# Packed attention and a mixture of experts on one core: the first matrix in 256-column chunks, quarters in the first beat

## The chip, the core and the metric

The kernel runs on one core of a Trainium2 chip. TensorE (PE in the profile, its weight loads PEld) multiplies, VectorE (DVE), ScalarE (ACT) and GpSimd (POOL) do the elementwise work, and SyncE (SP) issues nearly all DMAs from one queue. The metric is device microseconds of one execution, and the median of several runs is given.

## The reference

Each head's 32 "packed" queries `p` attend to 576 keys and values; then the 576 rows of `q` attend to the 32 packed rows. The result `x` (4608 tokens of 512 numbers, 8 batches of 576) goes through a mixture of 8 experts, one expert for each token.

```python
p_packed = sm_attn(p, k, v)               # 8 batches x 8 heads, 32 x 64 out
x = sm_attn(q, p_packed, p_packed)        # 8 x 8 x 576 x 64, heads side by side: 4608 x 512
logits = x @ w_gate; e_idx = argmax(logits)
gate_w = softmax(logits)[e_idx]; eom = sigmoid(x @ w_output_gate)
for e in range(8):
    mask = e_idx == e
    h = maximum(x[mask] @ w1[e], 0)       # 512 -> 1024
    out[mask] = gate_w * eom[mask, e] * (h @ w2[e])   # 1024 -> 512
```

## The kernel before

**A beat is a batch.** Since each `x` row is a weighted mean of 32 packed rows for each head, `x @ w1[e]` is never made from `x`: `values_up` multiplies the packed rows by the first matrix of the batch's commonest expert (`ps_G`, in the document G), and `ffn` multiplies the attention weights by G. Every operand is split into a high and a low part (`Gh`, `Gl`, `ah`, `al`, `w2h`, `w2l`), and a product is three matmuls. Tokens of the batch that chose another expert are marked and done later, in `quarters` and `first_leftover` (the left-over pass), which stages its own weights.

**The parts of a beat.** `encode` (scores `ps_s`, the sum over values `ps_pp`, its division `rs` and `ppc` on DVE, its transposition `ps_ppT` by PE, the expert's choice), `route` (scores of `q`, exponentials, `a2T`, the split into `ah` and `al`, the gate's logits `ps_lg`), `weights` (DMAs of the first matrix, tile `w`, four of 512 KB; of the second, tile `wst`, four of 512 KB; then for each of these an ACT cast to `w2h` and a subtraction to `w2l` on POOL or DVE), `values_up`, `ffn`. `ffn` has two halves: 256 tokens, then 320. In each, eight blocks of the 1024 hidden columns take six matmuls each into `ps_h`; ACT (L615) and DVE (L618) make `hT` from it; then `ps_o` is the product with the second matrix (L656, L671).

**The order is written by hand.** `ffn` of one batch is the backbone; `START` and, for each beat, a string of `PLANS` say after which of its steps a piece of another batch's `encode` (y, x, Y), `route` (t, r), `weights` (W, w), `values_up` (G, g) or of the left-over pass (l) is issued. Every engine runs its instructions in the order in which they are written, and so does SP's queue of DMAs. Before the first beat PE is kept busy by products of a blank tile (`warm`, `CFG["warm"]`, digits in `START`).

**Where the bounds come from.** PSUM has 8 banks in rotation: a new tile waits until the tile eight allocations before it is read. `by_head` and `beside` (L104) issue matmuls for four 32-row strips side by side. In the first beat G of 512 columns (a half) is made, split by ACT (`Gh`, L88) and DVE (`Gl`, L89), and the other half follows after two blocks of `ps_h`.

Of the kernel before, what the change touches and what calls it, by code (L numbers as in the profile page):

```python
# [22 lines left out]
           pool=("w2.2", "w3.3", "w4.3", "w5.3", "w6.3", "w7.3", "w3.0", "w4.0", "w5.0", "w6.0", "w7.0", "w0.0",  # L23
# [11 lines left out]
PLANS = ["0:kq 1:t 2:GGW 3:W 5:ty 6:W 7:tW 9:WWW 10:yW 11:tt 12:t 13:y 14:ytyy 15:qt 16:tyyyt 18:y "  # L35
# [5 lines left out]
        + [STEADY] * 2 + [  # L41
         "1:y 3:y 8:rxyr 9:Wyrrrrr 10:tqt 12:r 13:r 14:rr 15:yl 16:rw 17:wkl 18:v 19:vx 25:xx 26:lxwx "
         "29:l 30:kxw 31:wqgxgrlw 34:rrgwxwxwll",
         "1:yl 3:y 8:rxylr 9:Wyrrrrr 10:tqt 12:r 13:rl 14:rr 15:y 16:rw 17:wk 18:v 19:vx 25:xx 26:xwx "
         "30:kxw 31:wqgxgrlw 34:rrgwxwxw",
         "1:l 3:t 6:W 7:t 34:l"]

# [2 lines left out]
def tile_packed_attn_then_moe(ctx, tc, first_in, qT, kp, k2, v, w1, w2, out):  # L50
# [343 lines left out]
    def route(b):  # L394
# [40 lines left out]
        for part in ([0, 1],) if b else ([0], [1]):  # L435
            ts = slice(part[0] * HS, (part[-1] + 1) * HS)
            n = (ts.stop - ts.start) // NP
            sf = [x[:, ts] for x in rows]
            sv = [x.rearrange("p (j n) -> p j n", n=NP) for x in sf]
            sms = []  # L440
            for g in range(NG):
                mx = sb.tile([P, S // NP, 1], F32, tag="mx", name="mx", bufs=2)[:, :n]
                nc.vector.tensor_reduce(mx, sv[g], axis=AX.X, op=ALU.max)
                eng("sub", b, part[0], g).tensor_tensor(sv[g], sv[g], mx.to_broadcast([P, n, NP]), ALU.subtract)  # L444
                yield
            for g in range(NG):
# [118 lines left out]
    def values_up(b):  # L565

        w1s = W[b][0]
        ppT = packed[b]
        G[b] = []

        def up(n):
            banks = [bank("ps_G") for _ in range(NG)]
            by_head(banks, ppT, w1s[n * NPAIR:(n + 1) * NPAIR])
            return banks

        def take_in(banks):
            made = [[sb.tile([P, BANK], F32R, tag=x, name=x, bufs=4, **WIDE) for x in ("Gh", "Gl")] for _ in banks]
            step = BANK // 2 if b == 0 else BANK
            for x in range(0, BANK, step):
                for ps, (gh, gl) in zip(banks, made):  # L580
                    split(gh[:, x:x + step], gl[:, x:x + step], ps[:, x:x + step])
            G[b].extend(map(tuple, made))
# [141 lines left out]
    def leftover():  # L724
# [56 lines left out]
    def quarters(nb, m):  # L781
# [37 lines left out]
        vals = st([4], "l_valq")  # L819
        nc.vector.tensor_copy(vals, ps)  # L820
        ridi = row_ids(st, decf, vals, m)
        yield
        ps = bank("ps_l")[:, :NPAIR * m]
# [96 lines left out]
def _layout(q, k, v, p, moe_w_gate, moe_w_output_gate, moe_w1, moe_w2):  # L920
# [26 lines left out]
    def parts(x):  # L947
# [33 lines left out]
```

## Time and profile before

| | |
|---|---|
| median of 3 runs | 391.12 us (390.99 to 392.66) |
| the profiled execution, its own time | 389.64 us |
| span of its trace | 388.0 us |
| PE busy | 379.3 us, 98% of the span |
| DVE, ACT, POOL busy | 248.4, 186.2, 106.5 us |
| TensorE's granted clock | full in all 40 slices of the span |

The profiled execution is 1.6 us longer than its span and 1.5 us below the median. Busy times overlap and don't add up; PE's 98% says that its instructions follow one another nearly throughout. "Idle before" is time an engine stood still ahead of an instruction, with what released it; "issue" means that nothing that the profile shows was waited for. A wait of an engine other than PE costs only what it passes on.

### The profile page before, as it was taken

Reading aid. Unit: us, or ns where it says so; the run is one execution under the profiler, and the core shown is the slowest. Engines: PE = TensorE matmul, PEld = TensorE weight load, DVE = VectorE, ACT = ScalarE, POOL = GpSimd, SP = SyncE. Lnnn points to the kernel's source line nnn. Section 1 sums busy time; section 2 is a strip of 40 time slices with the busy share of each in tenths; the row PEclk is TensorE's granted clock in tenths of the full one; section 3 lists DMA queues with packets and bytes.
Section 4 is the critical chain, followed back from the end, with each engine's and each line's share of the span. In section 5 each row is a group of like instructions: output and inputs, shape, how many; then the busy total and the mean of one; then the engine's idle time right before and its main releaser. Section 6 shows DMA issues by size and latency. Waiting matters only on the chain.

```text
span 388.0 us, 9841 instructions
## 1 busy us (share of the span) xinstructions
PE 379.3 (98%) x3880; PEld 310.7 (80%) x3880; DVE 248.4 (64%) x703; ACT 186.2 (48%) x421; POOL 106.5 (27%) x92
## 2 busy tenths in 40 slices
PE   8799999999999999999999999999999999999996
PEld 3468886879769897798869898698968789788986
DVE  5778688775867973678646875559846594153250
ACT  2267444744395255734566346552476334552321
POOL 4534013232146021431044021340735101442000
PEclk9999999999999999999999999999999999999999
DMA  7899189909983499522894259712863948600101
GB/s 288 332 387 421 64 244 387 379 20 328 387 272 95 164 295 414 190 98 95 334 355 175 64 170 407 280 51 91 277 263 111 359 160 287 236 30 0 56 14 57
DMA packets 35535, 83.79 MB, mean 216 GB/s; under 512 B 3486, under 2 KB 15136, under 8 KB 35488
## 3 DMA queue, kind: packets, MB, share of 16 engines
q1 hardware_dynamic: 35024, 81.89, 57.9%
q10 hardware_dynamic: 432, 1.26, 0.8%
q8 instruction: 31, 0.51, 0.5%
q14 instruction: 16, 0.13, 0.1%
q0 software_dynamic: 32, 0.00, 0.0%
HBM read 67.93 MB, written 15.27 MB: 214 GB/s over the span
## 4 chain that ended last, share of the span: by engine, by line
PE 94%; DMA 3%; DVE 2%; issue 1%; ACT 0%; SPq 0%
PE ps_o L656 46%; PE ps_h L97 25%; PE ps_o L671 8%; PE ps_G L104 4%; PE ps_pp L104 3%; PE ps_s2T L104 2%; PE ps_s L104 2%; DMA w<-in_w_dram 2%; PE ps_lg L104 1%; PE warm L128 1%; DMA k<-in_first_dram 1%; PE ps_lo L853 0%; DVE a1T L333 0%; PE ps_ppT L352 0%; DVE nm L307 0%
## 5 line engine op out<-in xcount | busy, mean ns | idle before, releaser
L656 PE MATMUL ps_o<-w2h,hT 128*128 128x512 f32 (+1 forms) x528 | 165.7, 387 | 0.0
L656 PEld LDWEIGHTS ps_o<-w2h,hT 128*128 128x128 f32 x528 | 98.2, 188 | 22.8 <-issue 3.0
L656 PE MATMUL ps_o<-w2l,hT 128*128 128x512 f32 (+1 forms) x264 | 101.2, 383 | 0.0
L618 DVE SCALAR_TENSOR_TENSOR hT<-ps_h,hT 128x256 fp32r<-128x256 f32 x192 | 61.1, 352 | 53.9 <-ACT hT L615 53.2
L559 POOL TENSOR_TENSOR w2l<-wst,w2h 128x1024 fp32r<-128x1024 f32 x27 | 66.6, 2476 | 100.8 <-ACT w2h L557 97.5
L97 PE MATMUL ps_h<-ah,Gh 128*128 128x256 f32 (+1 forms) x256 | 77.1, 301 | 1.3 <-DVE hT L618 0.8
L97 PE MATMUL ps_h<-al,Gh 128*128 128x256 f32 (+1 forms) x256 | 75.7, 296 | 0.0
L97 PE MATMUL ps_h<-ah,Gl 128*128 128x256 f32 (+1 forms) x256 | 75.7, 296 | 0.0
L615 ACT ACTIVATE hT<-ps_h 128x320 fp32r<-128x320 f32 (+1 forms) x128 | 52.0, 414 | 39.4 <-PE ps_h L97 38.7
L656 PEld LDWEIGHTS ps_o<-w2l,hT 128*128 128x128 f32 x264 | 49.7, 188 | 9.0
L97 PEld LDWEIGHTS ps_h<-ah,Gh 128*128 128x128 f32 x256 | 48.5, 190 | 3.2 <-DVE hT L618 1.0
L97 PEld LDWEIGHTS ps_h<-al,Gh 128*128 128x128 f32 x256 | 48.5, 190 | 1.2 <-issue 0.7
L97 PEld LDWEIGHTS ps_h<-ah,Gl 128*128 128x128 f32 x256 | 48.5, 189 | 0.0
L557 ACT CAST w2h<-wst 128x1024 fp32r<-128x1024 f32 x32 | 33.3, 1063 | 7.0 <-DMA wst<-in_w_dram 7.0
L471 POOL TENSOR_TENSOR al<-a2T,ah 128x576 fp32r<-128x576 f32 (+1 forms) x10 | 14.2, 1423 | 81.0 <-ACT ah L468 80.9
L639 ACT ACTIVATE ob<-ps_o,scm_all 128x512 f32<-128x512 f32 (+1 forms) x28 | 19.1, 682 | 33.7 <-PE ps_o L656 33.2
L89 DVE TENSOR_TENSOR Gl<-ps_G,Gh 128x512 fp32r<-128x512 f32 (+1 forms) x36 | 20.9, 623 | 16.2 <-ACT Gh L88 15.9
L671 PE MATMUL ps_o<-w2h,hT 128*128 128x512 f32 x64 | 25.2, 393 | 0.0
L671 PE MATMUL ps_o<-w2l,hT 128*64 128x512 f32 x64 | 23.7, 391 | 0.0
L468 ACT CAST ah<-a2T 128x576 fp32r<-128x576 f32 (+1 forms) x18 | 11.1, 621 | 18.3 <-DVE a2T L462 18.3
L447 ACT ACTIVATE s<-s 128x576 f32<-128x576 f32 (+1 forms) x18 | 11.1, 629 | 16.6 <-DVE s L444 14.1
L88 ACT CAST Gh<-ps_G 128x512 fp32r<-128x512 f32 (+1 forms) x36 | 17.6, 542 | 2.2 <-PE ps_G L104 1.7
(175 smaller groups left out, 407.2 us busy)
## 6 DMA issues: line engine op xcount, KB each, us to landing
w<-in_w_dram SPq DMA_DIRECT2D x36, 512.0 KB, 5.8
wst<-in_w_dram SPq DMA_DIRECT2D x32, 512.0 KB, 9.1
vt<-in_v_dram SPq DMA_DIRECT2D x14, 650.0 KB, 11.5
q<-in_qT_dram SPq DMA_DIRECT2D x14, 576.0 KB, 4.6
out_dram<-ob SPq DMA_DIRECT2D x31, 256.0 KB, 2.3
a_d<-a2T SPq DMA_DIRECT2D x16, 320.0 KB, 3.1
k<-in_kp_dram SPq DMA_DIRECT2D x7, 640.0 KB, 6.8
k<-in_k_dram SPq DMA_DIRECT2D x7, 576.0 KB, 9.1
```

The costliest lines, as they stand in the source:

```text
L88: (hi_eng or nc.scalar.copy)(hi, src)
L89: (lo_eng or nc.vector).tensor_tensor(lo, src, f(hi), ALU.subtract)
L97: res = nc.tensor.matmul(dst, a, m, start=j == 0, stop=j == len(seq) - 1)
L104: res = nc.tensor.matmul(dst, a, m, start=j == 0, stop=j == len(seqs[0]) - 1)
L471: eng("al", b, part[0], g).tensor_tensor(al[:, g, ts], a2T[:, g, ts], f(ah[:, g, ts]), ALU.subtract)
L557: nc.scalar.copy(hi, st)
L559: eng("w", b, j).tensor_tensor(lo, st, f(hi), ALU.subtract)
L615: nc.scalar.activation(hT[:, :n], ps, AF.Relu)
L618: nc.vector.scalar_tensor_tensor(hT[:, d0:d0 + s1 - s0], ps[:, s0:s1], 0.0, f(hT[:, s0:s1]), op0=ALU.max, op1=ALU.subtract)
L639: nc.scalar.activation(ob[:, cs], ps[:, cs], AF.Copy, scale=sc)
L656: nc.tensor.matmul(ps[:, cs], a, m[:, cs], start=fc == i == 0, stop=fc == FC - 1 and i == 2)
L671: nc.tensor.matmul(ps[:n], a, m, start=i == 0, stop=i == len(seq) - 1)
```

## The change

The first matrix is laid out and staged as four chunks of 256 columns with all 512 rows (before: 512 columns and 256 rows, so that two chunks made a half of G). A chunk keeps its 512 KB. `by_head` is therefore called once for each chunk, with twice the matmuls of half the columns. In the first beat `values_up` yields after each quarter; the order of pieces in that beat, the order of the two head groups in the first half of `route`, three entries of the list of operations on POOL and one product of the blank tile are changed with it. In the left-over pass the DMAs of the first matrix are issued in step 31 of a beat, behind the pieces `g`, instead of step 34, and the product `ps_lv` with its copy becomes four strips in `ps_l`'s block.

```diff
-START = "kkvYY3qYYYvYqYY1kYkYYYYY4YtYYtYtWtWtv2tqvttv7qt5tvt6ttGkyG"
+START = "kkvYY3qYYYvYqYY1kYkYYYYY4YtYYtYtWtWtv2tqvttv7qt5tGGvttkyGG"
-PLANS = ["0:kq 1:t 2:GGW 3:W 5:ty 6:W 7:tW 9:WWW 10:yW 11:tt 12:t 13:y 14:ytyy 15:qt 16:tyyyt 18:y "
-         "19:y 21:ryt 22:y 23:dr 24:tyw 25:r 26:r 29:rw 30:r 31:r 32:rt 33:rr 34:rkgkrgg",
+PLANS = ["0:kGtGq 3:WWtGG 5:y 6:WWW 7:t 10:W 11:yWyt 13:ytW 14:yttqt 16:yytyytytt 17:y 21:d 22:ryy "
+         "25:rtry 26:wr 27:r 30:r 32:g 33:rkrtr 34:rgwrkrg",
...
-         "29:l 30:kxw 31:wqgxgrlw 34:rrgwxwxwll",
-         "1:yl 3:y 8:rxylr 9:Wyrrrrr 10:tqt 12:r 13:rl 14:rr 15:y 16:rw 17:wk 18:v 19:vx 25:xx 26:xwx "
+         "30:kxw 31:wqgxgrlwl 34:rrgwxwxwll",
+         "1:y 3:y 8:rxylr 9:Wyrrrrr 10:tqt 12:r 13:rl 14:rr 15:y 16:rw 17:wk 18:v 19:vx 25:xx 26:xwx "
...
+            ahead = (1, 0) if part == [0] else (0, 1)
-            for g in range(NG):
+            for g in ahead:
...
-        W[b] = ([st[:, c] for st in w1s for c in range(2)], [])
+        W[b] = ([stage(src) for src in w1c], [])
...
-        def up(n):
-            banks = [bank("ps_G") for _ in range(NG)]
-            by_head(banks, ppT, w1s[n * NPAIR:(n + 1) * NPAIR])
-            return banks
+        def up(j, banks):
+            x = j % 2 * QUART
+            by_head([ps[:, x:x + QUART] for ps in banks], ppT, [w1s[j][:, c] for c in range(NPAIR)])
...
         if b == 0:
-            for n in range(DF // BANK):
-                banks = up(n)
+            for j in range(Q):
+                banks = [bank("ps_G") for _ in range(NG)]
+                up(j, banks)
                 yield
-                take_in(banks)
+                if j % 2 == 0:
+                    rooms()
+                take_in(banks, j // 2, j % 2 * QUART, j % 2 * QUART + QUART)
                 yield
         else:
-            both = [up(n) for n in range(DF // BANK)]
+            both = [[bank("ps_G") for _ in range(NG)] for _ in range(DF // BANK)]
+            for j in range(Q):
+                up(j, both[j // 2])
...
-        ps = bank("ps_lv")[:, :4]
-        nc.tensor.matmul(ps, part["pick"], vals, start=True, stop=True)
...
-        w1=moe_w1.reshape(E, DM // (2 * P), 2, P, DF // BANK, BANK).transpose(0, 4, 1, 3, 2, 5).reshape(E, -1, P, 2, BANK),
+        w1=moe_w1.reshape(E, NPAIR, P, -1, BANK // 2).transpose(0, 3, 2, 1, 4),
```

**PE, first beat.** Here stands PE's order where the scores of the next batch (`ps_s`) end and the first `ps_h` begin. A row is an instruction as written; in the trace a strip's row of `ps_G` or `ps_s` is two matmuls with two weight loads, a `ps_h` row one with one. Before, two blocks (12 rows) of `ps_h`, then the second half of G:

```order
91 L97 MATMUL ps_h<-al,Gh 128x256
92 L97 MATMUL ps_h<-ah,Gl 128x256
93 L97 MATMUL ps_h<-ah,Gh 128x256
94 L97 MATMUL ps_h<-al,Gh 128x256
95 L97 MATMUL ps_h<-ah,Gl 128x256
96 L104 MATMUL ps_G<-w_360,ppT 32x512 x4
97 L104 MATMUL ps_G<-w_362,ppT 32x512 x4
98 L97 MATMUL ps_h<-ah,Gh 128x256
```

And in the changed kernel, the end of the scores, the second and third quarter of G, and eight rows of `ps_h`:

```order
80 L104 MATMUL ps_s_434<-k 32x144
81 L104 MATMUL ps_s_435<-k 32x144
82 L104 MATMUL ps_G<-w_358,ppT 32x256 x8
83 L104 MATMUL ps_G<-w_360,ppT 32x256 x8
84 L97 MATMUL ps_h<-ah,Gh 128x256
85 L97 MATMUL ps_h<-al,Gh 128x256
86 L97 MATMUL ps_h<-ah,Gl 128x256
87 L97 MATMUL ps_h<-ah,Gh 128x256
88 L97 MATMUL ps_h<-al,Gh 128x256
89 L97 MATMUL ps_h<-ah,Gl 128x256
90 L97 MATMUL ps_h<-ah,Gh 128x256
91 L97 MATMUL ps_h<-al,Gh 128x256
```

Three quarters of G now stand ahead of the first `ps_h`; the first quarter (`w_356`) stands ahead of the scores, the last (`w_362`) behind 18 rows of `ps_h`.

**PE, between the halves of the first beat.** `ps_pp` and `ps_ppT` belong to the next batch's `encode`, `ps_lg` to the beat's own `route`. Before:

```order
166 L656 MATMUL ps_o<-w2h,hT 128x512
167 L104 MATMUL ps_lg<-a2T,pg 32x160 x8
168 L104 MATMUL ps_pp<-vt,a1T 32x65 x40
169 L97 MATMUL ps_h<-ah,Gh 128x320
170 L97 MATMUL ps_h<-al,Gh 128x320
```

After the change:

```order
165 L661 MATMUL ps_o<-w2h,hT 128x512
166 L104 MATMUL ps_pp<-vt,a1T 32x65 x40
167 L104 MATMUL ps_lg<-a2T,pg 32x160 x8
168 L352 MATMUL ps_ppT<-ident,ppc 128x128
169 L97 MATMUL ps_h<-ah,Gh 128x320
```

The transposition `ps_ppT` stood behind 12 rows of `ps_h` (row 181 before) and now stands ahead of all of them.

**SP, end of the first beat.** These are the DMAs of the second batch's second matrix (`wst`) and what is issued around them. Before:

```order
50 L678 DMA out_dram<-ob 64x512
51 L543 ISA
52 L543 DMA wst<-in_w_dram 128x1024
53 L543 ISA
54 L543 DMA wst<-in_w_dram 128x1024
55 L543 ISA
56 L543 DMA wst<-in_w_dram 128x1024
57 L543 ISA
58 L543 DMA wst<-in_w_dram 128x1024
59 L640 DMA out_dram<-ob 128x512
60 L464 DMA a_d<-a2T 128x5x128 x2
61 L232 DMA k<-in_kp_dram 128x1280
```

After:

```order
50 L683 DMA out_dram<-ob 64x512
51 L645 DMA out_dram<-ob 128x512
52 L232 DMA k<-in_kp_dram 128x1280
53 L465 DMA a_d<-a2T 128x5x128 x2
54 L544 ISA
55 L544 DMA wst<-in_w_dram 128x1024
56 L544 ISA
57 L544 DMA wst<-in_w_dram 128x1024
```

Four DMAs (128x512, 128x1280 and twice 128x640 numbers of 4 bytes) now stand ahead of the four of `wst`.

## Rows read from the trace of the kernel before

**Rows 1.** The page, parts 1 and 3: busy time and count; queue, packets, MB.

```profile
PE 379.3 (98%) x3880; PEld 310.7 (80%) x3880; DVE 248.4 (64%) x703; ACT 186.2 (48%) x421; POOL 106.5 (27%) x92
...
q8 instruction: 31, 0.51, 0.5%
```

**Rows 2.** Timeline of PE, 15.5 to 27.6 us: start, length, instruction, count [idle before].

```profile
16.81 2.86 PE L128 MATMUL warm<-blank 128*128 128x128 f32 x9 [0.92 <-issue]
...
27.18 0.28 PE L97 MATMUL ps_h<-ah,Gh 128*128 128x256 f32 x1 [0.56 <-issue]
```

**Rows 3.** DMA table of 14.40 to 15.45 us: queue, packets, MB, share.

```profile
q8 instruction: 1, 0.02, 5.6%
```

**Rows 4.** DMA table of 24.70 to 25.80 us.

```profile
q8 instruction: 1, 0.02, 5.5%
```

**Rows 5.** Groups of PE's matmuls, 16.81 to 27.17 us: count after the x.

```profile
L104 PE MATMUL ps_G<-w,ppT 64*32 64x512 f32 x32 | 3.2, 601 | 0.0
...
L97 PE MATMUL ps_h<-ah,Gh 128*128 128x256 f32 x7 | 2.2, 312 | 0.0
...
L104 PE MATMUL ps_s<-k 64*32 64x144 f32 x64 | 1.9, 285 | 0.0
```

**Rows 6.** Timeline of PE, 19.5 to 26 us.

```profile
22.61 0.39 PE L97 MATMUL ps_h<-ah,Gh 128*128 128x256 f32 x1
...
24.25 1.09 PE L104 MATMUL ps_G<-w,ppT 64*32 64x512 f32 x16
```

**Rows 7.** Timeline of PE, 305 to 309 us.

```profile
304.73 1.07 PE L104 MATMUL ps_s2T<-q,ppT 64*32 64x288 f32 x32
```

**Rows 8.** Tile w, its DMA issued at 16.7 us: the third chunk.

```profile
L543 SPq DMA_DIRECT2D w<-in_w_dram x1: 332/332/332, 16.7 to 16.7; - x1
...
DMA to landing us min/median/max: 6.0/6.0/6.0
```

**Rows 9.** Timeline of ACT, 26 to 28 us.

```profile
26.89 1.05 ACT L557 CAST w2h<-wst 128x1024 fp32r<-128x1024 f32 x1
```

**Rows 10.** Timeline of PE, 30.2 to 45.2 us.

```profile
30.40 0.39 PE L656 MATMUL ps_o<-w2h,hT 128*128 128x512 f32 x1
...
41.40 0.75 PE L104 MATMUL ps_lg<-a2T,pg 128*32 128x160 f32 x16
41.97 1.32 PE L104 MATMUL ps_pp<-vt,a1T 128*32 128x65 f32 x80
...
45.08 0.27 PE L352 MATMUL ps_ppT<-ident,ppc 128*128 128x128 f32 x1
```

**Rows 11.** Timeline of DVE, 43 to 44 us.

```profile
43.35 0.16 DVE L343 TENSOR_SCALAR rs<-ps_pp 128x2 f32<-128x2 f32 x1 [1.82 <-PE ps_pp L104]
...
43.74 0.29 DVE L347 TENSOR_TENSOR ppc<-ps_pp,rs 128x128 f32<-128x128 f32 x1
```

**Rows 12.** Timeline of SP's queue, 59 to 67 us.

```profile
59.55 2.43 SPq L543 DMA_DIRECT2D wst<-in_w_dram  x4
...
66.18 3.12 SPq L232 DMA_DIRECT2D k<-in_kp_dram  x1
```

**Rows 13.** Tile wst, its DMAs issued from 59.5 us on.

```profile
DMA to landing us min/median/max: 7.7/8.8/10.2
```

**Rows 14.** Busy time by stretch: us, engines, PEclk, DMA share, GB/s.

```profile
60.00:70.00 10.00, 10.00 (x127) 6.69 (x125) 7.95 (x15) 5.06 (x9) 3.43 (x4) 1.00 1.02 387
```

**Rows 15.** Timeline of ACT, 69 to 73 us.

```profile
69.62 1.03 ACT L557 CAST w2h<-wst 128x1024 fp32r<-128x1024 f32 x1
71.77 0.21 ACT L291 ACTIVATE up<-nm 64x8 f32<-64x8 f32 x1 [1.11 <-DVE nm L311]
```

**Rows 16.** Timeline of PE, 72.5 to 74.5 us.

```profile
73.96 0.38 PE L97 MATMUL ps_h<-ah,Gh 128*128 128x256 f32 x1 [0.77 <-DVE hT L618]
```

**Rows 17.** Timeline of PE's weight loads, 305.5 to 308 us.

```profile
306.17 0.61 PEld L839 LDWEIGHTS ps_lh<-w,l_own 128*32 128x32 f32 x16 [0.25 <-DMA w<-in_w_dram]
307.44 0.58 PEld L839 LDWEIGHTS ps_lh<-w,l_own 128*32 128x32 f32 x12 [0.66 <-DMA w<-in_w_dram]
```

More of the change, by code (lines that the diff above doesn't have):

```diff
@@ L25 @@
                  "al6.0.1", "al7.0.1", "sub1.0.0", "w3.1", "w4.1", "w5.1", "w6.1", "w7.1", "al1.0.0", "al0.0.1",
[1 row of a table removed]
[1 row of a table added]
                  "w0.2", "mul2.0.1", "al2.0.0", "mul0.0.0"))
-START = "kkvYY3qYYYvYqYY1kYkYYYYY4YtYYtYtWtWtv2tqvttv7qt5tvt6ttGkyG"
+START = "kkvYY3qYYYvYqYY1kYkYYYYY4YtYYtYtWtWtv2tqvttv7qt5tGGvttkyGG"
 STEADY = ("1:y 3:y 8:rxyr 9:Wyrrrrr 10:tqt 12:r 13:r 14:rr 15:y 16:rw 17:wk 18:v 19:vx 25:xx 26:xwx "
           "30:kxw 31:wqgxgrw 34:rrgwxwxw")
-PLANS = ["0:kq 1:t 2:GGW 3:W 5:ty 6:W 7:tW 9:WWW 10:yW 11:tt 12:t 13:y 14:ytyy 15:qt 16:tyyyt 18:y "
[1 row of a table removed]
+PLANS = ["0:kGtGq 3:WWtGG 5:y 6:WWW 7:t 10:W 11:yWyt 13:ytW 14:yttqt 16:yytyytytt 17:y 21:d 22:ryy "
[1 row of a table added]
          "0:Wyyy 4:WW 5:yyyWy 6:vW 7:W 9:Wyyyt 10:yW 11:yt 12:t 13:rydy 15:tr 16:ryr 17:rq 20:r 21:q "
          "22:v 23:rwxx 24:wrx 26:kr 27:twr 28:r 29:v 31:xrx 32:rrvg 33:rw 34:wwgxwwg",
[2 rows of a table removed]
-        + [STEADY] * 2 + [
-         "1:y 3:y 8:rxyr 9:Wyrrrrr 10:tqt 12:r 13:r 14:rr 15:yl 16:rw 17:wkl 18:v 19:vx 25:xx 26:lxwx "
-         "29:l 30:kxw 31:wqgxgrlw 34:rrgwxwxwll",
-         "1:yl 3:y 8:rxylr 9:Wyrrrrr 10:tqt 12:r 13:rl 14:rr 15:y 16:rw 17:wk 18:v 19:vx 25:xx 26:xwx "
[2 rows of a table added]
+        + [STEADY] * 2 + ["1:y 3:y 8:rxyr 9:Wyrrrrr 10:tqt 12:r 13:r 14:rr 15:yl 16:rw 17:wkl 18:v 19:vx 25:xx 26:lxwx "
+         "30:kxw 31:wqgxgrlwl 34:rrgwxwxwll",
+         "1:y 3:y 8:rxylr 9:Wyrrrrr 10:tqt 12:r 13:rl 14:rr 15:y 16:rw 17:wk 18:v 19:vx 25:xx 26:xwx "
          "30:kxw 31:wqgxgrlw 34:rrgwxwxw",
@@ L69, in tile_packed_attn_then_moe @@
     MQ = P // Q
+    QUART = BANK // 2
     T8 = 8
@@ L466, in route @@
                 yield
-            for g in range(NG):
+            for g in ahead:
                 nc.scalar.copy(ah[:, g, ts], a2T[:, g, ts])
             yield
-            for g in range(NG):
+            for g in ahead:
                 eng("al", b, part[0], g).tensor_tensor(al[:, g, ts], a2T[:, g, ts], f(ah[:, g, ts]), ALU.subtract)
@@ L541, in stage @@
     def stage(src, tag="w1", by=nc.sync):
-        st = sb.tile([P, 2, BANK], F32, tag=tag, name=tag, bufs=CFG[tag], **EVEN)
+        st = sb.tile([P, 2 * BANK], F32, tag=tag, name=tag, bufs=CFG[tag], **EVEN).rearrange("p (c n) -> p c n", n=src.shape[2])
         by.dma_start(st, src)
@@ L549, in weights @@
         w1c, w2c = chunks(e)
-        w1s = [stage(src) for src in w1c]
-        W[b] = ([st[:, c] for st in w1s for c in range(2)], [])
+        W[b] = ([stage(src) for src in w1c], [])
         yield
@@ L569, in values_up, with rooms, take_in @@
         G[b] = []
-        def up(n):
-            banks = [bank("ps_G") for _ in range(NG)]
-            by_head(banks, ppT, w1s[n * NPAIR:(n + 1) * NPAIR])
-            return banks
[L576 to L582, printed above, removed]
+        def up(j, banks):
+            x = j % 2 * QUART
+            by_head([ps[:, x:x + QUART] for ps in banks], ppT, [w1s[j][:, c] for c in range(NPAIR)])
+        def rooms():
+            G[b].extend(tuple(sb.tile([P, BANK], F32R, tag=x, name=x, bufs=4, **WIDE) for x in ("Gh", "Gl")) for _ in range(NG))
+        def take_in(banks, n, c0=0, c1=BANK):
+            for g, ps in enumerate(banks):
+                gh, gl = G[b][n * NG + g]
+                split(gh[:, c0:c1], gl[:, c0:c1], ps[:, c0:c1])
         if b == 0:
-            for n in range(DF // BANK):
-                banks = up(n)
+            for j in range(Q):
+                banks = [bank("ps_G") for _ in range(NG)]
+                up(j, banks)
                 yield
-                take_in(banks)
+                if j % 2 == 0:
+                    rooms()
+                take_in(banks, j // 2, j % 2 * QUART, j % 2 * QUART + QUART)
                 yield
         else:
-            both = [up(n) for n in range(DF // BANK)]
+            both = [[bank("ps_G") for _ in range(NG)] for _ in range(DF // BANK)]
+            for j in range(Q):
+                up(j, both[j // 2])
             yield
-            for banks in both:
-                take_in(banks)
+            for n, banks in enumerate(both):
+                rooms()
+                take_in(banks, n)
                 yield
@@ L766, in leftover @@
             ps = bank("ps_lh")
-            product(ps, xT, w1c[n * NG:(n + 1) * NG])
+            for x in range(2):
+                for c in range(NPAIR):
+                    nc.tensor.matmul(ps[:, x * QUART:(x + 1) * QUART], xT[:, c], w1c[2 * n + x][:, c],
+                                     start=c == 0, stop=c == NPAIR - 1)
             nc.scalar.copy(h[:, n * nf:(n + 1) * nf], ps.rearrange("p (c n) -> p c n", n=P))
@@ L798, in quarters @@
         dec, decf = decoded(st, cur)
-        sizes = dict(a2=NG * m, pp=P, pick=P, a4=NG * NPAIR * m, x=NPAIR * m, hT=nf * P, h=fw)
+        sizes = dict(a2=NG * m, pp=P, pick=P, a4=NG * NPAIR * m, x=NPAIR * m + 4, hT=nf * P, h=fw)
         own, n0, part = raw(sum(sizes.values()), "l_own"), 0, {}
@@ L816, in quarters @@
         yield
-        ps = bank("ps_lv")[:, :4]
-        nc.tensor.matmul(ps, part["pick"], vals, start=True, stop=True)
[L819 to L823, printed above, removed]
+        ps = bank("ps_l")[:, :NPAIR * m + 4]
         strips = [slice(j * MQ, (j + 1) * MQ) for j in range(Q)]
-        beside([ps[j] for j in strips], [[(pp[:, j], a4[:, j.start // D])] for j in strips])
+        beside([ps[j, :NPAIR * m] for j in strips], [[(pp[:, j], a4[:, j.start // D])] for j in strips])
+        beside([ps[j, NPAIR * m:] for j in strips], [[(part["pick"][:, j], vals)] for j in strips])
         nc.scalar.copy(xT, ps)
-        xT = xT.rearrange("p (c n) -> p c n", n=m)
+        xT, vals = xT[:, :NPAIR * m].rearrange("p (c n) -> p c n", n=m), xT[:, NPAIR * m:]
         yield
@@ L837, in quarters @@
             for j in range(Q):
-                n, f0 = divmod(j * fw, BANK)
-                nc.tensor.matmul(ps[j * MQ:(j + 1) * MQ], xT[:, c], w1c[n * NG + c // 2][:, c % 2, f0:f0 + fw],
-                                 start=c == 0, stop=c == NPAIR - 1)
+                nc.tensor.matmul(ps[j * MQ:(j + 1) * MQ], xT[:, c], w1c[j][:, c], start=c == 0, stop=c == NPAIR - 1)
         nc.scalar.activation(h, ps, AF.Relu)
@@ L855, in quarters @@
         yield
+        ridi = row_ids(st, decf, vals, m)
         ob = sb.tile([P, dw], F32, tag="ob", name="l_ob", bufs=CFG["ob"])
```

6 rows, old and new, of tables (PLANS, pool) are left out of this document.

## The prediction

> **What bounds the kernel now.** I read the page first: PE works 379.3 of 388.0 us [rows 1], so the time is PE's own work plus its few stalls, and an edit counts only by PE's work, PE's stalls, or a stall it adds. Then I went through PE's timeline for gaps. Two stand in the region that the change rewrites: 0.92 us ahead of 16.81 and 0.56 us ahead of 27.18 [rows 2]. Both are put down to "issue", so no semaphore and no data explains them. The reader is to see what lies between them. There stand 9 products of the blank tile [rows 2], 32 matmuls of `ps_G`, 64 of `ps_s` and three groups of 7 `ps_h`, of which one is shown [rows 5]: 9 + 32 + 64 + 21 = 126 matmuls, and as many weight loads, 252 instructions. The page has a DMA queue called "instruction" with 31 packets of 16 KB [rows 1]; PE's 3880 matmuls and 3880 loads over 31 are 250 to a packet. So the stalls stand one packet apart.
>
> The packets' times fit. One lies within 24.70 to 25.80; its share there, 5.5% of 16 engines over 1.10 us, is 0.97 us on one engine, so it ended between 25.67 and 25.80 [rows 4], 1.4 to 1.5 us before PE went on at 27.18 [rows 2]. One lies within 14.40 to 15.45; 5.6% of 16 engines over 1.05 us is 0.94 us, so it ended between 15.34 and 15.45 [rows 3], 1.4 to 1.5 us before PE went on at 16.81 [rows 2]. My reading: at 16.81 and 27.18 PE had run out of fetched code, and went on 1.4 us after the next 16 KB had arrived. No time of the second packet's request is shown; the packet is late because it shares engines that move bulk DMAs all this time.
>
> **The change, part by part.** *The chunks.* A half of G becomes two quarters: 32 matmuls of 256 columns for 16 of 512. PE's columns stay the same, and I cost the form at nothing: the half took 1.09 us [rows 6], while 32 matmuls of the same strips with 288 columns take 1.07 [rows 7]. So 32 of 256 take no longer, and a quarter takes about 0.5 us. A tenth of a microsecond either way for each of the 16 halves, 1.6 us in all, is what those two rows can't exclude.
>
> *The first beat.* What matters is where the end of the fetched code falls. It still begins at 16.81, since nothing before it changes. Now count: 7 blank products (one product, two matmuls, is dropped), 16 for the first quarter, 64 `ps_s`, 32 for the second and third quarter: 119. The 126 are full after 7 `ps_h`, where before 21 `ps_h` and all of G were behind PE by then. The eighth row of `ps_h` in the first piece of the changed order is where PE runs dry.
>
> When is it there? The third quarter waits for the third chunk: issued at 16.7, landed 6.0 later, at 22.7 [rows 8]; with 0.5 us for the quarter the first `ps_h` starts near 23.2, where it started at 22.61 [rows 6]. A `ps_h` takes 0.119 us: 48 - 21 = 27 of them fill 27.18 [rows 2] to 30.40, where `ps_o` starts [rows 10]. Seven end at 24.0. The same DMAs are issued ahead at the same times, so I let the packet come when it came. PE then stands from 24.0 to 27.18, some 3.1 us, five times the idle of before. Left are 41 `ps_h` (4.88 us) and the last quarter (0.5): 32.56. One more wait follows: the last quarter's `Gh` on ACT now stands behind a cast of 1.05 us [rows 9], while PE has only three blocks to go before it needs it. Between nothing and the whole 1.05 I take 0.3, since three blocks (2.1 us) cover most of cast and split. `ps_o` starts at 32.86 instead of 30.40: **+2.45**. Bounds: the packet 1.5 us earlier or later gives +1 to +4; and if it is not late at all, 23.2 + 48 x 0.119 + 0.5 + 0.3 = 29.7, a gain of 0.7.
>
> Against this stands a rule. The Trainium skill's page "Runtime: NRT & Kernel Launch", section "Instruction fetch mechanics", says that the engine's sequencer fetches the next 16 KiB block (256 instructions) through a DMA queue of its own while it runs the current one, and that the cost of crossing is "mostly hidden". The size agrees with the 252 counted here; the hiding does not at 16.81 and 27.18, where 0.92 and 0.56 us are lost. By the rule the first beat would give -0.7, by the rows +2.45.
>
> *pp, lg, ppT.* The chain from `ps_pp` over DVE to `ps_ppT`: `rs` starts at 43.35, `ppc` at 43.74 and lasts 0.29 to 44.03 [rows 11], 0.76 us after the end of `ps_pp` (41.97 + 1.32 = 43.29, rows 10). Before, 12 `ps_h` covered it (`ps_ppT` at 45.08). Now only `ps_lg` does, 41.97 - 41.40 = 0.57 us [rows 10]. PE waits the rest and a little for the signal: **+0.3** (0.2 to 0.5).
>
> *The second batch's `wst`.* Before, issued at 59.55 [rows 12], first one landed 7.7 later [rows 13], at 67.25, 2.4 us before ACT's cast at 69.62 [rows 15]. Now four DMAs stand ahead: 128 x 4 B x (512 + 1280 + 2 x 640) = 1.57 MB, at 387 GB/s with the DMA engines full [rows 14] 4.1 us. It can't be issued before the second `a_d`, right behind which `k` went at 66.18 [rows 12]. So it lands near 71.3, and the cast ends at 72.35. Behind the cast on ACT stands `up` (L291), which started at 71.77 [rows 15]; it is the head of a chain of small DVE and ACT steps behind which `hT` and then PE wait: PE already stands 0.77 us there, to 73.96 [rows 16]. That stall grows by 72.35 - 71.77 = **+0.6**. Bounds: nothing, if the queue drains faster than the mean, and 1.6 (the cast's whole length and half a microsecond) if it lands a microsecond later.
>
> *Left-over pass.* PE's loads of `ps_lh` stood 0.25 and 0.66 us for the chunks [rows 17]. Issued behind `g` in step 31 the chunks come earlier. What was lost on PE itself is less than the loads' 0.91, as matmuls still run; I take half: **-0.45** (0 to -0.9). `ps_lv` going and four small strips coming is under 0.1 us, as is the swapped order in `route`: in the first beat the POOL, DVE and ACT steps end before PE gets to them, hidden by the idle at the packet. If that is gone, the al of one group on POOL could hold the second `ps_h` by some tenths.
>
> *The rest.* Batches 2 to 7 have PE without gaps at the places touched; PE's work is unchanged and a delay once made is kept. Sum: 2.45 + 0.3 + 0.6 - 0.45 = **+2.9 us**. Profile: 389.64 + 2.9 = 392.5. That execution was 1.5 us under the median of 391.12, so a median near **394.0**.
>
> **The rivals.** *The code comes in time* (0.25). If the request follows PE's position, or its packet finds a gap in the bulk, PE doesn't stand: -0.7 + 0.3 + 0.6 - 0.45 = -0.25, a median near 390.9: not slower. For it: the other packets, 29 of 31, cost no stall that I found. Against: both packets that were fetched under the first bulk loads did. It decides where the packet ends before 24.0 - 1.4 = 22.6, some 3 us earlier than in the trace of before. It is what the rule of the Trainium skill's page named above would make of the time.
>
> *The gains add up* (0.12). As the last, and PE's stall at 73.96 goes as well (0.77) since `wst` is in time, and the left-over waits go wholly (0.9): -0.7 + 0.3 - 0.77 - 0.9 = -2.1, a median near 389.0. Against it: `up` waits for DVE there, which no edit speeds up.
>
> *The clock* (0.05). Three idle microseconds are three times the longest of before, during which the granted clock stayed full (1.00 in rows 14, as in the stretches around the two stalls). If it falls to the lower level (1.2 of 2.4 GHz) for as long as the idle lasted, 3 us of work take 6: +3 more, near 397. No row shows it.
>
> **How the numbers follow.** My forecast, 392.5 to 395.5, has 0.55; 0.03 is for what I don't see. A measurement of this kernel tells about 0.5%, 2 us, from no change. Slower by more than that (over 393.1): the forecast but for its lower edge, and the clock: 0.58. Within: the code in time, and the lower edge: 0.29. Faster (under 389.2): 0.13. The range reaches from 389.4, just above the second rival, leaving some 0.1 below, to 396.8, leaving some 0.08 above.
>
> **What would show it.** In the profile after: one PE gap put down to "issue" ahead of the eighth `ps_h`, near 24.0, ending near 27.2, 1.4 us behind a packet of the instruction queue; `ps_o` starting near 32.9; a gap of 0.3 us ahead of `ps_ppT`; a gap of 1.4 us instead of 0.77 where `hT` releases PE in the second beat, with the cast between `nm` and `up` on ACT; no wait for `w` in `ps_lh`. The prediction is wrong if the packet of 24.8 comes by 22.6, or if the quarter-wide matmuls cost more than half of a half.

## The result, and the profile after

The changed kernel takes 394.23 us (median of 20 runs, 391.77 to 397.7) against 391.06 (20 runs, 389.17 to 395.54): a ratio of 1.0082 (95% interval 1.0061 to 1.0103), so it is slower, by 3.2 us. The forecast was 394.0. The sum was right; of its four terms only the smallest, the 0.3 ahead of `ps_ppT`, was. In seven of the 20 runs TensorE's mean granted clock was 0.999 or 1.000 and the time 391.77 to 393.57 us; in the other thirteen the clock was 0.987 to 0.996 and the time 393.67 to 397.70.

The profiled execution took 395.58 us, 1.35 above the median, with a span of 393.9 against 388.0. As the profiled execution of before lies 1.4 us below its median, the two traces differ by 5.9 us, 2.7 more than the medians. The page of the changed kernel, lines of parts 1 to 3, first:

```profile
PE 380.1 (96%) x4140; PEld 315.9 (80%) x4140; DVE 251.0 (64%) x701; ACT 186.0 (47%) x421; POOL 106.5 (27%) x93
...
PEclk9999999899999999999999999999999999999999
...
q8 instruction: 33, 0.54, 0.5%
```

PE is busy 0.8 us longer than before [rows 1], so 5.1 of the 5.9 us are time in which it stands still. (A lower clock shows in the 0.8, and so does the dropped blank product, which took 0.65.) The instruction queue has 33 packets for 31: the narrow products of G are 256 more matmuls and as many loads. PE's timeline in the first beat (start, length, instruction, count, idle before), with the DMA table of 22.90 to 24.10 us behind it:

```profile
16.81 2.21 PE L128 MATMUL warm<-blank 128*128 128x128 f32 x7 [0.92 <-issue]
...
22.60 0.67 PE L104 MATMUL ps_G<-w,ppT 64*32 64x256 f32 x16 [0.60 <-DMA w<-in_w_dram]
...
24.01 0.28 PE L97 MATMUL ps_h<-ah,Gh 128*128 128x256 f32 x1
25.38 0.28 PE L97 MATMUL ps_h<-al,Gh 128*128 128x256 f32 x1 [1.09 <-issue]
...
31.24 0.40 PE L661 MATMUL ps_o<-w2h,hT 128*128 128x512 f32 x1
```

```profile
q8 instruction: 1, 0.02, 5.2%
```

The seventh `ps_h` starts at 24.01 and the gap stands ahead of the eighth, as the count said. It ends 1.4 us behind an instruction packet (5.2% of 16 engines over 1.20 us is 1.00 us on one engine; it ended between 23.9 and 24.1). But this packet came some 1.7 us earlier than that of [rows 4], so `ps_o` starts at 31.24, only 0.84 later than in [rows 10]. Next the second batch's `ps_pp`, then its G, on PE; behind them G's line of before:

```profile
42.24 1.34 PE L104 MATMUL ps_pp<-vt,a1T 128*32 128x65 f32 x80
43.40 0.73 PE L104 MATMUL ps_lg<-a2T,pg 128*32 128x160 f32 x16
44.48 0.30 PE L352 MATMUL ps_ppT<-ident,ppc 128*128 128x128 f32 x1 [0.36 <-DVE ppc L347]
```

```profile
63.90 0.66 PE L104 MATMUL ps_G<-w,ppT 64*32 64x256 f32 x16
64.88 0.67 PE L104 MATMUL ps_G<-w,ppT 64*32 64x256 f32 x16 [0.32 <-DMA w<-in_w_dram]
66.69 0.67 PE L104 MATMUL ps_G<-w,ppT 64*32 64x256 f32 x16 [1.14 <-DMA w<-in_w_dram]
67.84 1.11 PE L104 MATMUL ps_G<-w,ppT 64*32 64x256 f32 x16 [0.48 <-DMA w<-in_w_dram]
...
79.38 0.39 PE L97 MATMUL ps_h<-ah,Gh 128*128 128x256 f32 x1 [0.78 <-DVE hT L623]
```

```profile
65.42 1.95 PE L104 MATMUL ps_G<-w,ppT 64*32 64x512 f32 x32
```

`ps_ppT` waits 0.36 us, as forecast. The three waits for `w`, 1.94 us, were in no term. Where `hT` releases PE [rows 16], 73.96 has become 79.38: 5.42 us later, of which 0.84 came from the first beat and some 0.3 from `ps_ppT`, so 4.3 us were lost between. The gap there is 0.78 as before; the forecast growth is not there. From the last quarter of G on the clock was lower (stretches: us, busy times, granted clock, DMA share, GB/s):

```profile
64.00:68.00 4.00, 2.06 (x56) 0.64 (x63) 3.44 (x6) 2.22 (x4) 0.65 (x1) 0.98 1.02 382
68.00:70.00 2.00, 2.00 (x19) 1.00 (x14) 1.72 (x2) 0.97 (x2) 1.58 (x3) 0.50 1.07 361
70.00:72.00 2.00, 2.00 (x8) 1.57 (x7) 0.94 (x2) 0.11 (x1) 0.00 (x0) 0.69 1.11 414
```

At 0.50 and 0.69 of the full 2.4 GHz, the lower level for most of 68 to 72, PE did in 4 us what takes 2.4 at full clock. So 1.6 of the 4.3 us are the clock's; the others were lost in G, with its waits for `w`. The last part is the sixth batch, with the left-over pass: PE, then DVE, then POOL:

```profile
305.95 0.30 PE L352 MATMUL ps_ppT<-ident,ppc 128*128 128x128 f32 x1 [1.08 <-DVE ppc L347]
...
312.39 1.96 PE L841 MATMUL ps_lh<-w,l_own 128*32 128x256 f32 x32
```

```profile
298.92 0.31 DVE L490 TENSOR_TENSOR g_oh<-L,g_mx 128x40 f32<-128x40 f32 x1
299.27 2.44 DVE L493 TENSOR_TENSOR g_ohq<-g_oh,in_quarter 128x160 fp32r<-128x160 f32 x1
```

```profile
296.80 4.73 POOL L559 TENSOR_TENSOR w2l<-wst,w2h 128x1024 fp32r<-128x1024 f32 x2
```

`ps_lh` runs without a wait now (32 in one row; [rows 17] shows the two waits of before). But `ps_ppT` waits 1.08 us for `ppc`, which stands in DVE's order behind `g_ohq`; that one took 2.44 us, and ended 0.18 us after POOL's pair of `w2l` products, which ended at 301.53.

### The profile page after: what moved, and what is told of

Read it like the earlier page. It is cut to its first block, busy times and chain, and to the rows that moved or that the text cites. A ratio compares the mean times of both kernels' runs of the same rounds, so it can differ in the third digit from the quotient of the medians.

```text
span 393.9 us, 10367 instructions
## 1 busy us (share of the span) xinstructions
PE 380.1 (96%) x4140; PEld 315.9 (80%) x4140; DVE 251.0 (64%) x701; ACT 186.0 (47%) x421; POOL 106.5 (27%) x93
## 4 chain that ended last, share of the span: by engine, by line
PE 88%; DVE 4%; DMA 4%; issue 1%; SPq 1%; ACT 0%
PE ps_o L661 42%; PE ps_h L97 25%; PE ps_o L676 7%; DMA w<-in_w_dram 3%; PE ps_G L104 3%; PE ps_pp L104 3%; PE ps_s2T L104 2%; PE ps_s L104 1%; PE ps_lg L104 1%; DMA k<-in_first_dram 1%; DVE g_ohq L493 1%; SPq L544 1%; PE ps_lh L841 0%; PE ps_lo L854 0%; DVE s L426 0%
## 5 line engine op out<-in xcount | busy, mean ns | idle before, releaser
L472 POOL TENSOR_TENSOR al<-a2T,ah 128x576 fp32r<-128x576 f32 (+1 forms) x9 | 13.2, 1472 | 81.5 <-ACT ah L469 81.5
L89 DVE TENSOR_TENSOR Gl<-ps_G,Gh 128x512 fp32r<-128x512 f32 (+1 forms) x36 | 20.9, 623 | 16.7 <-ACT Gh L88 16.5
L104 PE MATMUL ps_G<-w,ppT 64*32 64x256 f32 x512 | 17.5, 389 | 3.2 <-DMA w<-in_w_dram 2.8
```

Of the source, the lines that this page charges most:

```text
L89: (lo_eng or nc.vector).tensor_tensor(lo, src, f(hi), ALU.subtract)
L104: res = nc.tensor.matmul(dst, a, m, start=j == 0, stop=j == len(seqs[0]) - 1)
```

## The experiments

Each is timed against the kernel before on the same chip; the ratio is to that one. Three chips were used, so two variants are best compared by their ratios.

**The same kernel again (same).** No edit.

> The changed kernel once more, unedited, to see which of its gaps come back in a second profile. If the gaps belong to the order of instructions, PE stops again ahead of the eighth ps_h of the first beat near 24.0 us with about 1 us idle, again waits for the tile w in the second beat's G with 1.5 to 2.5 us idle near 64 to 68 us, and again runs at the lower clock for some 2 us behind it. If the waits for w, the lower clock or the 1.1 us gap ahead of ps_ppT near 305 us were chance of one execution, they are gone or halved here. Ratio to the kernel before 1.006 to 1.010.

Ratio 1.0119 (1.0077 to 1.0162), above the expected 1.010. The code gap stands ahead of the eighth `ps_h` again, with 0.52 us; the waits for `w` in the second batch come back (1.84 us in all), the gap ahead of `ps_ppT` too (0.97); the lower clock does not. So the waits belong to the order; the clock falls in some executions only. Two lines of PE, the first `ps_o` and `hT`'s release:

```profile
32.52 0.40 PE L661 MATMUL ps_o<-w2h,hT 128*128 128x512 f32 x1
...
79.01 0.39 PE L97 MATMUL ps_h<-ah,Gh 128*128 128x256 f32 x1 [0.78 <-DVE hT L623]
```

At full clock throughout, the second batch takes 46.49 us between these two lines, where it took 43.56 before (30.40 in [rows 10] to 73.96 in [rows 16]). The first beat ends 2.1 us later than before, but 1.35 of that arose ahead of the changed order: `ps_e`, just ahead of the blank products, starts at 16.64 instead of 15.29.

**G of the second batch later (g_late).**

```diff
-         "25:rtry 26:wr 27:r 30:r 32:g 33:rkrtr 34:rgwrkrg",
+         "25:rtry 26:wr 27:r 30:r 33:rkrtr 34:rgwrkrgg",
```

> One edit to the changed kernel: the piece that makes the second batch's G goes back from step 32 to step 34 of the first beat, to the row of PE's order where it stood before the change; all else stays changed. Theory (the loss is a wait for the second batch's first matrix, and the lower clock that follows it): the wait shrinks from 1.9 us of idle to under 0.6, the clock stays full, and the kernel is 2.5 to 4 us faster than the changed one, ratio to before 0.998 to 1.003. Rival (the loss is the code fetch of the first beat, carried on): G waits less but the end moves by less than 1 us, ratio still 1.006 or more.

Ratio 1.0105 (1.0084 to 1.0126): the theory was wrong in its price. The rival's number came out, though not for its reason. The waits for `w` are gone, but PE stands at `hT`'s release instead. PE's and ACT's timelines, second batch:

```profile
78.63 0.38 PE L97 MATMUL ps_h<-ah,Gh 128*128 128x256 f32 x1 [3.30 <-DVE hT L623]
```

```profile
75.37 1.04 ACT L557 CAST w2h<-wst 128x1024 fp32r<-128x1024 f32 x1 [3.49 <-DMA wst<-in_w_dram]
76.44 0.21 ACT L291 ACTIVATE up<-nm 64x8 f32<-64x8 f32 x1
```

The cast waits 3.49 us for `wst`, and the chain that begins with `up` stands behind it: 3.30 us of idle on PE where there were 0.77 [rows 16]. It is the step that was priced at 0.6, and it is worth 2.5. In the changed kernel it does not show: PE has lost that time already, waiting for `w`, when it gets there. In this execution the clock also fell twice, behind the code gap (0.60 and 0.55 in 25 to 29 us) and behind the 3.30 us (0.50 and 0.65 in 80 to 84).

**Both back (beat1_old).** The edit of g_late, and the piece `w` that issues `wst` moved ahead:

```diff
-         "25:rtry 26:wr 27:r 30:r 32:g 33:rkrtr 34:rgwrkrg",
+         "25:rtry 26:wr 27:r 29:w 30:r 33:rkrtr 34:rgrkrgg",
```

> The changed kernel with G of the second batch back at step 34 (as in g_late) and, besides, the four DMAs of that batch's second matrix back ahead of k and a_d in SP's queue, where they stood before the change. Theory (the second batch's loss is two waits that take turns, for w where G stands early, for wst where it stands late): neither the wait for w in G nor the 3.5 us step ahead of hT's release near 75 us is left, that step is 0.9 to 1.2 us as before the change, and the kernel is 2 to 2.5 us faster than the changed one; ratio to before 1.003 to 1.007, with the code gap and the gap ahead of ps_ppT left. Rival (wst lands late whatever its place, because the DMA engines are full): the step stays above 2 us and the ratio above 1.008.

Ratio 1.0028 (1.0003 to 1.0052): by the ratios 2.1 us off the changed kernel's loss, as the theory had it, though a wait for `w` is left. PE waits 0.50 us for `w` in G and 0.79 ahead of `hT`'s release:

```profile
70.19 0.67 PE L104 MATMUL ps_G<-w,ppT 64*32 64x256 f32 x16 [0.50 <-DMA w<-in_w_dram]
...
77.48 0.39 PE L97 MATMUL ps_h<-ah,Gh 128*128 128x256 f32 x1 [0.79 <-DVE hT L623]
```

**The first beat's order back (first_old).** `START`, the first string of `PLANS`, `ahead`, the list for POOL and the blank product as before; pieces `G` doubled, since G has quarters now:

```diff
-START = "kkvYY3qYYYvYqYY1kYkYYYYY4YtYYtYtWtWtv2tqvttv7qt5tGGvttkyGG"
+START = "kkvYY3qYYYvYqYY1kYkYYYYY4YtYYtYtWtWtv2tqvttv7qt5tvt6ttGGGkyG"
-PLANS = ["0:kGtGq 3:WWtGG 5:y 6:WWW 7:t 10:W 11:yWyt 13:ytW 14:yttqt ...
+PLANS = ["0:kq 1:t 2:GGGGW 3:W 5:ty 6:W 7:tW 9:WWW 10:yW 11:tt 12:t ...
```

> The changed kernel with the first beat's order put back: START, the first string of PLANS, the order of the two head groups, the operations on POOL and the dropped blank product as before; the chunks of 256 columns and the left-over pass stay changed. Theory (the loss is in the order of the first beat): ratio 0.996 to 1.001, with the left-over pass alone left to help or hurt. Rival (narrow chunks cost by themselves, in every batch): ratio 1.004 or more. By the count of instructions PE should run out of code after 126 matmuls from 16.8 us on: 9 blank, 32 of G, 64 ps_s, 12 ps_h and 9 matmuls of the third quarter of G; so the gap put down to issue stands inside that quarter, not ahead of a ps_h.

Ratio 1.0057 (1.0037 to 1.0077): the theory's range missed, the rival's met, but not in every batch as the rival had it. The gap stands exactly where the count puts it, 9 matmuls into the third quarter of G:

```profile
16.46 2.86 PE L128 MATMUL warm<-blank 128*128 128x128 f32 x9 [0.92 <-issue]
...
23.79 0.64 PE L104 MATMUL ps_G<-w,ppT 64*32 64x256 f32 x9
26.21 1.06 PE L104 MATMUL ps_G<-w,ppT 64*32 64x256 f32 x23 [1.78 <-issue]
```

So with the old order the narrow chunks alone put 16 matmuls and 16 loads of the first half of G ahead of the point at which the code runs out, and the gap grows from 0.56 [rows 2] to 1.78 us. From the first `ps_o` (32.18) to `hT`'s release this execution takes 43.62 us, before 43.56, and G of the second batch 1.96 us, before 1.95; behind that the left-over pass gives back 0.8. So in this trace narrow chunks cost nothing in the later batches.

```profile
67.23 1.96 PE L104 MATMUL ps_G<-w,ppT 64*32 64x256 f32 x64
...
75.80 0.38 PE L97 MATMUL ps_h<-ah,Gh 128*128 128x256 f32 x1 [0.77 <-DVE hT L623]
```

This execution, at 390.67 us, is the fastest of the ten, 2.0 below their median, and the clock is not why: six of the ten ran at full clock and took up to 393.81. What the others lose beyond this trace is not shown.

**Same columns, more code (code_more).**

```diff
-            k = min(n, BANK // P)
+            k = min(n, BANK // P if i != 5 else 1)
```

> The changed kernel with the two blank products of 512 columns ahead of G written as eight of 128: the same columns, but 12 more matmuls and 12 more weight loads ahead of G; the columns and the data are the same. Theory (PE runs out of fetched code at a fixed count of instructions): the gap put down to issue leaves the eighth ps_h and stands after the 11th of the 16 matmuls of the third quarter of G, or a matmul or two beside that; PE goes on about 1.4 us behind an instruction packet as before, with 12 matmuls less done, so the first ps_o is 1 to 1.5 us later for the same packet time. Rival (the gap hangs on the data or the bank of that ps_h): it stays ahead of the eighth ps_h.

Ratio 1.0159 (1.0104 to 1.0213; four runs). The gap left the `ps_h` and stands after the 11th matmul of the third quarter:

```profile
22.92 0.64 PE L104 MATMUL ps_G<-w,ppT 64*32 64x256 f32 x11 [1.41 <-DMA w<-in_w_dram]
26.07 1.07 PE L104 MATMUL ps_G<-w,ppT 64*32 64x256 f32 x5 [2.50 <-issue]
27.07 0.58 PE L97 MATMUL ps_h<-ah,Gh 128*128 128x256 f32 x1
```

Nothing of the data or the columns was changed, so the place of the gap hangs on the count of instructions: this is the test that settles what "issue" was. `ps_o` starts at 35.89, much later than expected, for behind the gap the clock stayed at 0.50 from 26 to 32 us.

**Later bulk (after_later).** In the first batch five more reads of the expert's number between the second and the third chunk:

```diff
-        W[b] = ([stage(src) for src in w1c], [])
+        w1s = [stage(src) for src in w1c[:2]]
+        for _ in range(5 * (b == 0)):
+            e = nc.sync.value_load(estar_i[0:1, b, 0:1], min_val=0, max_val=E - 1)
+            w1c, w2c = chunks(e)
+        w1s += [stage(src) for src in w1c[2:]]
+        W[b] = (w1s, [])
```

> The changed kernel with one edit: in the first batch SP reads the expert's number five more times between the second and the third chunk of the first matrix, so that chunks three and four, and the DMAs behind them, are issued some 2 us later. Theory (the code packet is served behind the bulk DMAs that are already issued when PE enters the block, near 17 us): the packet that came at 22.8 to 24.8 us in all profiles so far comes 1.5 to 3 us earlier, and the gap put down to issue ahead of the eighth ps_h shrinks below 0.5 us or is gone, while the third chunk, now later, holds the third quarter of G by up to 1.5 us. Rival (the packet comes a fixed time after PE's entry, or with PE's position): it comes 6 to 8 us behind the entry as before, and the gap stays.

Ratio 1.0076 (1.0041 to 1.011). The packet came within 20.70 to 21.90 us and the code gap is gone, as the theory had it. But the third chunk, which went out at 19.88 instead of 16.73, now holds PE for 2.49 us, more than the code did, and the ratio stays. The DMA table of 20.70 to 21.90 us, then PE:

```profile
q8 instruction: 1, 0.02, 5.7%
```

```profile
24.20 1.11 PE L104 MATMUL ps_G<-w,ppT 64*32 64x256 f32 x16 [2.49 <-DMA w<-in_w_dram]
```

**The left-over pass put back (left_old), and alone (left_only).** left_old takes the strings of `PLANS` for the last batches back (`31:wqgxgrlw`, and `1:yl`); left_only is the kernel before with these strings of the change and without `ps_lv`.

> The changed kernel with the left-over pass's DMAs put back from step 31 to step 34 (and the last of them to step 1 of the next beat), as before the change; the product that left stays away. Theory (issued behind G they save PE's wait in ps_lh): PE waits again for w in ps_lh, about 0.7 us, and the kernel is 0.5 to 1 us slower than the changed one, less what the gap ahead of ps_ppT near 305 us (1.1 us) gives back if it hangs on these DMAs. Rival (the left-over pass's move brings nothing, as the gap ahead of ps_ppT takes it back): equal or faster by 0.5 us.

> The kernel before with the left-over pass's part of the change alone (DMAs of the first matrix in step 31 behind G, no product ps_lv of its own); chunks of 512 columns and the first beat as before. Theory (this part takes away PE's wait for w in ps_lh): 0.5 to 0.8 us faster than before, ratio 0.998 to 0.999, no gap in ps_lh. Rival (the earlier DMAs delay something in the same beat that PE then waits for, as the 1.1 us gap ahead of ps_ppT in two of the profiles may be): ratio 1.000 or more, with that gap.

left_old: 1.0138 (1.011 to 1.0166), with PE's waits in `ps_lh` back; 1.0 us above `same` in the median, though the gap ahead of `ps_ppT` is gone; the intervals of the two overlap. left_only: 0.9971 (0.9942 to 1.0001), by the ratio 1.1 us under before, its interval just reaching 1; no gap ahead of `ps_ppT` and none in `ps_lh`:

```profile
306.57 1.96 PE L834 MATMUL ps_lh<-w,l_own 128*32 128x256 f32 x32
```

**Less code (left_less).** left_only with two blank products dropped (`qt5tvt6ttGkyG` to `qttvtttGkyG`).

> As left_only, and two of the blank products ahead of G are left out (512 + 512 and 384 columns: six matmuls and six weight loads fewer, no part of the result). Theory (code runs out by count): the gap put down to issue moves six ps_h later, so it shrinks by up to 0.7 us or is gone, and the kernel is about 1.2 us faster than before, ratio 0.996 to 0.998. Rival (PE's idle time ahead of G lowers its clock): the clock falls below 1.00 between 17 and 24 us and the kernel is slower than left_only.

Ratio 0.9991 (0.9965 to 1.0017), 1.6 us above left_only in the median, though the intervals overlap; no gain, as the rival had it. The code gap is gone, but PE stood idle ahead of G (1.56 us) and worked at 0.64 and 0.51 of its clock in the stretches of 19 to 23 us. The profile of left_only shows a lower clock too (0.53 and 0.62 in 17 to 21 us), but the mean clock was under 0.998 in two of its twelve executions and in all twelve of left_less.

```profile
19.00:21.00 2.00, 1.53 (x12) 0.48 (x20) 1.12 (x4) 0.43 (x1) 0.67 (x2) 0.64 1.03 397
21.00:23.00 2.00, 2.00 (x48) 1.36 (x36) 1.10 (x3) 0.83 (x3) 1.73 (x2) 0.51 1.01 404
```

**Later bulk in the old layout (later), and the changed kernel mended (mended).** later is left_only with the five reads; mended is beat1_old with them and with `ps_ppT` back behind two blocks (`16:yytyytytt 17:y` to `16:yytyyttt 18:y 19:y`).

> The kernel before with the left-over pass's part of the change (as left_only) and the same five reads of the expert's number between the second and the third chunk. If the code packet is served behind the bulk that is issued ahead of it, the gap put down to issue (0.6 us, near 27 us) is gone and the kernel is 0.3 to 0.7 us faster than left_only where the third and fourth chunk still come in time for the second half of G; ratio 0.994 to 0.998. Rival: the gap stays, and the later chunks cost up to 1 us; ratio 0.998 or more.

> The changed kernel with its three waits taken away: G of the second batch and the DMAs of its second matrix where they stood before the change (as beat1_old), ps_ppT behind two blocks of ps_h as before, and the five reads of the expert's number. Theory (these are the whole loss): no gap ahead of ps_ppT near 45 us, the step ahead of hT's release near 75 us under 1.1 us, the code gap under 0.5 us, and a time at or below the kernel before, ratio 0.995 to 1.000. Rival (something else in the narrow chunks or the order costs): ratio above 1.002.

later: 0.9966 (0.9938 to 0.9994), the lowest of all, though left_only's 0.9971 lies in its interval, and not by its theory: the packet came as late as ever (within 24.9 to 26.1 us) and the gap stands at 0.3 us. mended: 0.9991 (0.996 to 1.0022); no code gap (packet within 20.4 to 21.6 us), no wait for `ppT`, and the step ahead of `hT`'s release as before. PE's wait for the third chunk is the longest left:

```profile
24.00 0.67 PE L104 MATMUL ps_G<-w,ppT 64*32 64x256 f32 x16 [2.57 <-DMA w<-in_w_dram]
```

Without the three waits the changed kernel is level with the kernel before, its interval reaching from 0.4% below to 0.2% above. It is not ahead, though the left-over pass alone brings some 1 us: the first `ps_o` still starts 1.0 us late (31.42), since the reads that brought the code earlier hold the third chunk back.

## Why the prediction was right, and which steps were not

The profiles, cut at two places that all of them have (us; the first beat's end is the first `ps_o`, the second batch ends with `hT`'s release):

| | first beat, to `ps_o` | second batch | rest |
|---|---|---|---|
| before | 30.40 | 43.56 | 314.0 |
| after | 31.24 | 48.14 | 314.5 |
| same | 32.52 | 46.49 | 314.2 |
| g_late | 32.16 | 46.47 | 314.7 |
| beat1_old | 32.58 | 44.90 | 313.1 |
| first_old | 32.18 | 43.62 | 313.2 |
| mended | 31.42 | 43.47 | 313.3 |
| left_only | 31.36 | 43.61 | 313.0 |

**The code (+2.45): right in mechanism and place, mis-sized.** The gap moved to the eighth `ps_h`, the 9th and the 11th matmul of a quarter as the instructions ahead of it were changed: one count, 126 matmuls with their loads, explains all three and before. In all ten profiles that have this gap PE goes on 1.2 to 1.4 us behind the end of the packet. The size was taken from the packet's time in one execution and from PE's arrival at 24.0. In the profiles of the changed order the packet came between 22.8 and 24.4, not at 24.8, and the idle is 0.5 to 1.7 us (0.52 in `same`, 1.73 in g_late) rather than 3.1. It is least in `same`, where the packet came latest: there PE came late too, held by the third chunk, which landed near 24.3. What the forecast left over for a rival, the lower clock, came instead in some of the profiles: after the code gap it was at 0.60 and 0.55 in 25 to 29 us in g_late, and full throughout in `same`. In the profile of after this term is 0.84 us, in g_late, with the lower clock, 1.8.

**`ps_ppT` (+0.3): right**, 0.36 us of waiting.

**The second batch (+0.6): the step that failed.** The forecast followed `wst` alone and took PE's work there as unmoved, though the piece `g` of the first beat's string goes from step 34 to 32. G of the second batch stands 12 `ps_o` earlier on PE (18 behind it ahead of the scores, 6 before) while its four chunks are issued 1.5 us later (57.70 for 56.20 on SP), and so it waits for `w`: 1.94 us of idle in after, 1.84 in `same`. What that costs by `hT`'s release is 2.6 us in `same`, at full clock (46.49 - 43.56, less 0.3 for `ps_ppT`), and 4.3 with the lower clock of after. The wait for `wst` was there too, and worth 2.5 us rather than 0.6; behind the wait for `w` it is hidden. Undoing one uncovers the other (g_late), undoing both brings 2.1 us (beat1_old).

**Left-over pass (-0.45): right in sign, too small.** It is worth 1.1 us alone by the ratio (left_only), and in the table's last column 0.7 to 1.0 in the four profiles that have it and no gap ahead of `ps_ppT`, g_late apart, whose clock fell there. In the changed kernel's own two profiles that gap, 1.08 and 0.97 us, takes it back.

**The sum.** Too much for the code, too little for the second batch and for the left-over pass, and the errors offset each other: 2.9 forecast, 3.2 measured between the medians. Read from the two profiled executions the terms come to 5.9 us, not 3.2; which of them is smaller in a median execution is not shown. The rival "the code comes in time" did not occur. "The clock", put at a chance of 0.05, did in part: thirteen of the 20 executions had a lower mean clock, and their median is 2.65 us above that of the other seven (395.47 and 392.82). The forecast held no such term. So the range was met, and the number rests on luck.

The Trainium skill's page "Runtime: NRT & Kernel Launch", section "Instruction fetch mechanics", has the cost of crossing a block as "mostly hidden". At the two blocks that are fetched while the first bulk loads run it is not: 0.92 and 0.56 us before, 0.92 and 1.09 after.

**Open.** What sets the time of the code packet: it came 2 to 4 us earlier in after_later and mended, where chunks three and four were issued later, and not in later, with the same reads. So bulk that stands ahead of it is not the whole reason.

## What to carry to other kernels

Gaps of the matrix engine that are put down to "issue", lie an equal number of instructions apart and end a fixed time behind a packet of the instruction queue are code that has not arrived; here splitting matmuls in two moved them, so count instructions from gap to gap before a change that adds some. Where pieces are moved in a hand-written order, follow every piece of the string on every engine: a wait that is taken away may only have covered the next one, and undoing one edit at a time then shows nothing. A gap can also cost behind itself, by a lower clock.

## What the runs showed that was not expected

In the sixth batch a DVE product that met POOL's pair of `w2l` products ended only when the pair had. In the changed kernel it is `g_ohq`, a product of 128x160: 0.32 us at seven of its eight places, 2.44 here. Its line's durations (least, median, most, in ns), first before, then after:

```profile
L492 DVE TENSOR_TENSOR g_ohq<-g_oh,in_quarter x8: 324/324/328, 44.8 to 340.4; 128x160 fp32r<-128x160 f32 x8
```

```profile
L493 DVE TENSOR_TENSOR g_ohq<-g_oh,in_quarter x8: 324/325/2442, 45.1 to 346.3; 128x160 fp32r<-128x160 f32 x8
```

In after_later it is the product ahead of it, `g_oh`, with 2.17 us; before, `g_oh` started 0.12 us after the pair and took 0.20. DVE and POOL of after_later, then of before:

```profile
298.62 2.17 DVE L490 TENSOR_TENSOR g_oh<-L,g_mx 128x40 f32<-128x40 f32 x1
```

```profile
295.99 4.75 POOL L564 TENSOR_TENSOR w2l<-wst,w2h 128x1024 fp32r<-128x1024 f32 x2
```

```profile
293.60 0.20 DVE L489 TENSOR_TENSOR g_oh<-L,g_mx 128x40 f32<-128x40 f32 x1
```

```profile
288.73 4.75 POOL L559 TENSOR_TENSOR w2l<-wst,w2h 128x1024 fp32r<-128x1024 f32 x2
```

In the twelve profiles other than that of before, one of the two products met the pair each time, took 0.56 to 2.44 us, and ended 0.05 to 0.18 us after it. This also tells when `ps_ppT` waits in that batch: DVE was held for 2.0 to 2.2 us in `same`, after and after_later, the three that have the gap, and for under 1.3 us in the others; the gap (0.97, 1.08, 0.83) is the hold less some 1.15 us. That POOL held DVE is read from these times; no run moved the pair alone, and why it came later against DVE than before is open.

And the clock: of seven code gaps of 0.5 to 2.5 us in the changed layout, four were followed by stretches at the lower clock (g_late, beat1_old, left_old, code_more) and three, of 0.52, 1.09 and 1.78 us, were not (same, after, first_old), so what one execution shows of it should not be priced as certain.
